# Loading the inputs of a gated linear attention a batch at a time instead of a chunk at a time

## The chip, the cores and the metric

The kernel runs on one core of one Trainium2 chip. The metric is the device time of one execution in microseconds (us), the median over several runs. Engines are named as in the profile: PE (TensorE matmuls), PEld (its weight loads), DVE (VectorE), ACT (ScalarE), POOL (GpSimd), SP (SyncE, which here only issues transfers).

## The reference

A gated linear recurrence for each of 4 batches and 8 heads over 768 steps, and an MLP mixer over its output. All inputs and the output are float32.

```python
batch, n_heads, seq, head_dim = (4, 8, 768, 48)
state = alpha[:, :, t, :, None] * state + np.einsum('bhd,bhe->bhde', k[:, :, t], v[:, :, t])
y[:, :, t] = np.einsum('bhd,bhde->bhe', q[:, :, t], state)
...
# x: y as (batch, seq, heads * head_dim) = (4, 768, 384)
xt = x.transpose(0, 2, 1)
h = np.maximum(xt @ w_tok1, 0.0) @ w_tok2        # (768, 256), (256, 768)
u = x + h.transpose(0, 2, 1)
h2 = np.maximum(u @ w_ch1, 0.0) @ w_ch2          # (384, 1536), (1536, 384)
return (u + h2).astype(np.float32)
```

## The kernel before

The sequence is cut into chunks of 128 steps, six a batch, 24 in all; n is the chunk's number, and a chunk is worked on with its 128 steps on the partitions and 8 heads x 48 channels along them. The functions of one chunk:

- `load(n)` issues four transfers on SP, one for each of `at` (alpha), `kt`, `qt` and `vt`: 128 partitions of 8 rows, a row being the 48 float32 (192 bytes) of one head and step. The tiles come from the pool `inp` with NIN = 8 buffers for each name.
- `s_ln` (L132) takes the logarithm of alpha on ACT into `la`. `s_cum` (L138 to L157) sums it over the steps with matmuls into `ps_cum`; ACT makes `a_sb` and `ia_sb` by two exponentials; POOL multiplies `kt` to `pkk` and casts `vt` to `vb`, and makes `acqm`; `qt` is multiplied to `pkq` on DVE in batch 0 and on POOL after it.
- `s_tr` (L169, L171) transposes `pkk` and `pkq` by eight matmuls into `ps_tp`, copied to `tp` (by DVE in batch 0, by ACT after it).
- `s_gt` (L180, L183) makes the 128 x 128 products `gt_ps` of the eight heads, and DVE masks them to `gtm`.
- `s_y` (L193 to L215) makes the state product `ps_s` (it uses the same one buffer as `gt_ps`), from which DVE makes the state `ss`, then the output `ps_y`, which ACT copies to `x_sb`.

The mixer of a batch needs its six `x_sb`. It is a queue of units: tok1 (L229, 12 matmuls of 128 x 384), tok2 (L238, 12, with `u_sb` by DVE), utp (L247, transposes of u to `ut`), ch1 (L259, 72 matmuls into 12 tiles `rt`, with the maximum by ACT and DVE in turn) and ch2 (L269, 72 matmuls, with `o_sb` by DVE and the store by SP at L273). `fill` emits some units behind each step of the next batch's chunks, so that PE works on batch b's mixer during batch b + 1's scan; three ch2 units of a batch are held back and put between the units of the next mixer.

A scheduler reorders what the code emits, engine by engine; every engine then runs its own list in order.

The order of transfers is partly written by hand. The weights are cast to bfloat16 by transfers that POOL issues (L112): `wt1` and `wt2` when chunk 4 of batch 0 has its `vb`, `wc1` and `wc2` when chunk 5 has. `gates[n]` is the `vb` cast of chunk n. At the start six chunks are loaded; the `at` load of chunk 6 waits for `gates[5]`, and from then on loads run seven chunks ahead. Since `kt` and `qt` of chunk 6 stand ahead of that wait on SP, they are loaded before it.

## Time and profile before

| | |
|---|---|
| time, median of 3 runs | 210.76 us (208.86 to 211.78) |
| span of the profiled execution | 208.4 us |
| its own time | not shown beside its span; the three runs lie 0.5 to 3.4 us above the span |
| mean granted TensorE clock | 0.959 |
| busy | PE 174.2 us (84%), DVE 105.0, ACT 85.8, POOL 62.9 |
| transfers | 106,322 packets, 26.99 MB, 100,288 packets under 512 bytes |
| input loads | 96 of 192 KB, 3.7 to 3.8 us from issue to landing in the median |

A row of a timeline has the start in us from the span's beginning, the length, engine, line, operation, tile written <- tiles read, shape and count; in brackets stands how long the engine was idle before it, and what ended that. A row of the waits has who waited for whom, the sum in us, how often, and the longest. Slices are fortieths of the span, 5.2 us each, in tenths.

### The profile page before, as it was taken

What the parts mean: (1) busy time and instruction counts of PE and PEld (TensorE: products, weight loads), DVE (VectorE), ACT (ScalarE), POOL (GpSimd) and SP (SyncE); (2) the same over time, 40 slices, a digit from 0 to 9 for tenths busy, and PEclk for the clock granted to TensorE, in tenths of its full rate; (3) what the DMA queues carried; (4) which work ended last, traced back from release to release, by engine and by line L of the source; (5) the groups of instructions that cost most, each with busy time, mean ns of one, the idle gap of its engine ahead of it and who ended that gap; (6) DMA issues with size and microseconds to landing.
All of it is one profiled execution on the core that took longest, in us unless ns stands there. A gap on an engine that the chain in (4) does not pass through costs nothing.

```text
span 208.4 us, 4139 instructions
## 1 busy us (share of the span) xinstructions
PE 174.2 (84%) x1616; PEld 111.5 (53%) x1616; DVE 105.0 (50%) x179; ACT 85.8 (41%) x171; POOL 62.9 (30%) x104
## 2 busy tenths in 40 slices
PE   1276669232799999989999999999999999999993
PEld 0154445111475566646666666667656665656661
DVE  1277554103357455438765664378656446555321
ACT  3442221040526773685167744642667310054000
POOL 2543166004450441583245234551444000000000
PEclk9999999958559999999999999999999999999999
DMA  7999939999999998999989802111100021110132
GB/s 142 220 220 212 182 40 175 208 182 198 191 222 218 188 223 167 226 237 212 235 198 220 165 1 78 39 38 42 38 5 0 35 82 38 40 39 0 38 113 75
DMA packets 106322, 26.99 MB, mean 129 GB/s; under 512 B 100288, under 2 KB 105920, under 8 KB 106304
## 3 DMA queue, kind: packets, MB, share of 16 engines
q1 hardware_dynamic: 103296, 23.60, 53.7%
q0 software_dynamic: 3008, 3.15, 9.2%
q8 instruction: 12, 0.20, 0.4%
q14 instruction: 6, 0.05, 0.1%
HBM read 25.17 MB, written 4.72 MB: 143 GB/s over the span
## 4 chain that ended last, share of the span: by engine, by line
PE 59%; issue 12%; DMA 10%; ACT 8%; POOL 6%; SPq 2%; DVE 1%; POOLq 0%; ACTq 0%
PE ps_mm L269 20%; PE ps_mm L259 19%; DMA at<-in_alpha_dram 10%; ACT tp L171 4%; PE ps_tp L169 4%; PE ps_mm L238 4%; PE gt_ps L180 3%; PE ps_tp L247 2%; PE ps_mm L229 2%; SPq L124 2%; PE ps_y L207 1%; ACT a_sb L144 1%; PE ps_cum L138 1%; PE gt_ps L196 1%; POOL vb L154 1%
## 5 line engine op out<-in xcount | busy, mean ns | idle before, releaser
L259 PE MATMUL ps_mm<-ut,wc_152 128*128 128x384 bf16 x288 | 53.4, 330 | 1.2 <-DVE rt L264 0.5
L269 PE MATMUL ps_mm<-wc_153,rt 128*128 128x384 bf16 x288 | 50.9, 326 | 0.0
L264 DVE TENSOR_SCALAR rt<-ps_mm 128x384 bf16<-128x384 f32 x48 | 26.5, 555 | 22.9 <-PE ps_mm L259 22.6
L183 DVE TENSOR_TENSOR gtm<-gt_ps,u_107 128x1024 bf16<-128x1024 f32 x24 | 29.3, 1220 | 15.7 <-PE gt_ps L180 15.7
L269 PEld LDWEIGHTS <-rt 128*128 128x128 bf16 x288 | 27.1, 98 | 16.9
L259 PEld LDWEIGHTS <-wc_152 128*128 128x128 bf16 x288 | 26.8, 99 | 17.4 <-issue 1.5
L262 ACT ACTIVATE rt<-ps_mm 128x384 bf16<-128x384 f32 x48 | 23.1, 497 | 23.8 <-PE ps_mm L259 23.8
L215 ACT ACTIVATE x_sb<-ps_y 128x384 bf16<-128x384 f32 x24 | 11.8, 492 | 39.3 <-PE ps_y L211 35.2
L272 DVE TENSOR_TENSOR o_sb<-ps_mm,u_sb 128x384 f32<-128x384 f32 x24 | 13.3, 556 | 28.7 <-PE ps_mm L269 28.7
L154 POOL CAST vb<-vt 128x384 bf16<-128x384 f32 x24 | 12.8, 532 | 35.4 <-issue 23.6
L171 ACT COPY tp<-ps_tp 128x1024 bf16<-128x1024 bf16 x18 | 18.3, 1017 | 7.0 <-PE ps_tp L169 6.7
L144 ACT ACTIVATE a_sb<-ps_cum 128x388 f32<-128x388 f32 x24 | 11.9, 495 | 18.6 <-PE ps_cum L141 13.0
L241 DVE TENSOR_TENSOR u_sb<-ps_mm,x_sb 128x384 bf16<-128x384 f32 x24 | 12.0, 550 | 14.2 <-PE ps_mm L238 14.0
L180 PE MATMUL gt_ps<-tp 48*128 48x128 bf16 x192 | 11.9, 241 | 4.6 <-DVE tp L171 2.4
L180 PEld LDWEIGHTS <-tp 48*128 48x128 bf16 x192 | 6.4, 102 | 13.6 <-ACT tp L171 5.9
L146 ACT ACTIVATE ia_sb<-ps_cum 128x384 f32<-128x384 f32 x24 | 11.7, 487 | 0.0
L149 POOL TENSOR_TENSOR pkk_128<-kt,ia_sb 128x384 bf16<-128x384 f32 x8 | 7.9, 993 | 11.7 <-ACT ia_sb L146 11.7
L238 PE MATMUL ps_mm<-ht,wt_151 128*128 128x384 bf16 x48 | 11.4, 374 | 0.0
L229 PE MATMUL ps_mm<-x_sb,wt_150 128*128 128x384 bf16 x48 | 10.1, 342 | 0.6 <-ACT x_sb L215 0.6
L207 PE MATMUL ps_y<-vb,gtm 128*128 128x48 bf16 x192 | 9.6, 192 | 0.9 <-DVE gtm L183 0.9
L151 POOL TENSOR_TENSOR pkq_125<-qt,a_sb 128x384 bf16<-128x384 f32 x6 | 6.0, 996 | 14.3 <-ACT a_sb L144 14.3
L157 POOL TENSOR_TENSOR acqm<-a_sb,bm 128x8 f32<-128x8 f32 x24 | 5.5, 230 | 14.9 <-ACT a_sb L144 13.8
(91 smaller groups left out, 204.3 us busy)
## 6 DMA issues: line engine op xcount, KB each, us to landing
at<-in_alpha_dram SPq DMA_DIRECT2D x24, 192.0 KB, 3.7
kt<-in_k_dram SPq DMA_DIRECT2D x24, 192.0 KB, 3.8
qt<-in_q_dram SPq DMA_DIRECT2D x24, 192.0 KB, 3.8
vt<-in_v_dram SPq DMA_DIRECT2D x24, 192.0 KB, 3.8
out_dram<-o_sb SPq DMA_DIRECT2D x24, 192.0 KB, 1.9
wc_152<-in_moe_w_ch_dram POOLq DMA_DIRECT2D x1, 1152.0 KB, 10.1
wc_153<-in_moe_w_ch_dram POOLq DMA_DIRECT2D x1, 1152.0 KB, 17.2
wt_150<-in_moe_w_tok_dram POOLq DMA_DIRECT2D x1, 384.0 KB, 5.3
```

Source lines behind the costliest of these rows:

```text
L144: act.activation(a_sb, ps_cum[:, 0 : HD + 4], AF.Exp)
L154: gates[n] = gps.tensor_copy(vb, c["vt"])
L171: (act.copy if n >= NCH else dve.tensor_copy)(tp, ps_tp)
L180: pe.matmul(gt_ps[:, 4 * (h % 2) + j, :], lhsT=tp[base : base + D, 4 + j, :], rhs=tp[base : base + D, j, :], start=True, stop=True)
L183: dve.tensor_tensor(gtm, gt_ps, mask_b, ALU.mult)
L229: pe.matmul(ps, lhsT=wt1[:, kc, m * 128 : (m + 1) * 128], rhs=x[kc], start=(kc == 0), stop=(kc == NS - 1))
L238: pe.matmul(ps, lhsT=wt2[:, kc, i * 128 : (i + 1) * 128], rhs=ht[kc], start=(kc == 0), stop=(kc == NDT - 1))
L259: pe.matmul(ps, lhsT=wc1[:, kc, mc * 128 : (mc + 1) * 128], rhs=ut[kc][:, cs], start=(kc == 0), stop=(kc == NM - 1))
L262: act.activation(t[:, cs], ps, AF.Relu)
L264: dve.tensor_scalar_max(t[:, cs], ps, 0.0)
L269: pe.matmul(ps, lhsT=rt[mc][:, i * 128 : (i + 1) * 128], rhs=wc2[:, mc, :], start=(mc == 0), stop=(mc == NDC - 1))
L272: dve.tensor_tensor(t, ps, u[i], ALU.add)
```

## The change

`load` takes a batch instead of a chunk. Each of its four transfers brings all 48 rows of a partition (8 heads x 6 chunks) into a tile whose rows stand 64 float32 (256 bytes) apart; the chunks read their part of it through a view. `inp` has 2 buffers for each name, `rt` 13 instead of 24, and `o_sb` 3 instead of 4. Batch 0 is loaded at the start, batch b + 1 at the fifth chunk of batch b. The wait on `gates[5]` stands at the `at` load of batch 1. In DRAM the rows of one head lie together, and the built program takes four of them in one piece of 768 bytes; before, each row was a piece.

```diff
-    NIN = 8
+    NIN = 2
     inp = pool("inp", NIN)
...
-    rtpool = pool("rtpool", 24)
-    opool = pool("opool", 4)
+    rtpool = pool("rtpool", 13)
+    opool = pool("opool", 3)
...
-    def load(n):
-        b, ci = divmod(n, NCH)
-        c = ctxs[n] = {"b": b, "ci": ci}
-        ts = ci * C
+    PAD = 64
+
+    def load(b):
+        ts = {}
         for name, src in (("at", alpha), ("kt", k), ("qt", q), ("vt", v)):
-            t = inp.tile([128, H, D], F32, name=name)
-            d = nc.sync.dma_start(t, src[b, :, ts : ts + C, :].transpose([1, 0, 2]))
-            if n == NCH and name == "at":
+            t = inp.tile([128, H * NCH, PAD], F32, name=name)
+            d = nc.sync.dma_start(
+                t[:, :, 0:D], src[b].rearrange("h (c p) d -> p (h c) d", p=C))
+            if b == 1 and name == "at":
                 after(d, gates[NCH - 1])
-            c[name] = t
+            ts[name] = t.rearrange("p (h c) d -> p h c d", c=NCH)
+        for ci in range(NCH):
+            c = ctxs[b * NCH + ci] = {"b": b, "ci": ci}
+            for name, t in ts.items():
+                c[name] = t[:, :, ci, 0:D]
...
-    AHEAD = NIN - 1
     if True:
-        for n in range(NCH):
-            load(n)
-        loaded = NCH
+        load(0)
...
-            while n + 1 >= NCH - 1 and loaded < min(NT, n + 1 + AHEAD):
-                load(loaded)
-                loaded += 1
+            if ci == NCH - 2 and b + 1 < B:
+                load(b + 1)
```

The scheduler's order moves with it. On PE the sums of chunks 0 to 3 now come first; a first tok1 matmul of batch 0 stands ahead of the transposes of chunk 5; all of tok2 of batch 0 stands ahead of chunk 6, and two more sums and all u transposes ahead of chunk 6's state product. On POOL the three first `vb` come after the three first `pkk`, and for batch 1 `pkq`, `acqm` and `pkk` of chunks 6 to 8 and `pkq` of chunk 9 come before the `vb` of chunk 6. On SP the stores of batch 0 and the loads of batch 3 take turns.

## The prediction

> **What bounds the kernel now.** I read the page's slices first, then two windows of the span, then the waits, and last the timeline of the first 60 us.

> ```profile
> span 208.4 us, 4139 instructions
> PE   1276669232799999989999999999999999999993
> PEclk9999999958559999999999999999999999999999
> q0 software_dynamic: 3008, 3.15, 9.2%
> HBM read 25.17 MB, written 4.72 MB: 143 GB/s over the span
> wt_150<-in_moe_w_tok_dram POOLq DMA_DIRECT2D x1, 384.0 KB, 5.3
> ```

> The windows (columns: length, then busy time and count of PE, PEld, DVE, ACT, POOL, then clock, DMA share, GB/s):

> ```profile
> 0.00:58.00 58.00, 29.71 (x280) 19.99 (x281) 23.76 (x46) 17.11 (x36) 21.24 (x40) 0.89 1.01 180
> 58.00:205.00 147.00, 144.47 (x1337) 91.52 (x1337) 80.66 (x133) 68.68 (x136) 41.69 (x64) 0.99 0.49 111
> ```

> From 58 us to 205 us PE is busy for 144.47 of 147 us: TensorE bounds that stretch, and no input load can shorten it. Before 58 us PE works for 29.71 us only, while the DMA engines are full (share 1.01). So the change is decided by when the kernel reaches the state that it has at 58 us: the first state product of batch 1 (chunk 6, L196), behind which there is always mixer work for PE. From the waits:

> ```profile
> PE ps_cum L138 <- ACT la_123 L132: 5.9, 1, 5.9
> PE ps_cum L138 <- ACT la_124 L132: 4.1, 1, 4.1
> ```

> and from the timeline:

> ```profile
> 33.29 0.37 SPq L124 DMA_DIRECT2D at<-in_alpha_dram  x1
> ...
> 38.04 0.49 ACT L215 ACTIVATE x_sb<-ps_y 128x384 bf16<-128x384 f32 x1 [4.49 <-PE ps_y L211]
> ...
> 44.43 0.52 ACT L132 ACTIVATE la_123<-at 128x384 bf16<-128x384 f32 x1 [5.89 <-DMA at<-in_alpha_dram]
> ...
> 51.96 0.52 ACT L132 ACTIVATE la_124<-at 128x384 bf16<-128x384 f32 x1 [5.44 <-DMA at<-in_alpha_dram]
> ...
> 57.97 0.50 PE L196 MATMUL gt_ps<-vb,pkk_128 128*128 128x96 bf16 x4 [0.17 <-DVE gtm L183]
> ```

> Batch 0's scan is over at 38.04 (last x_sb). Then PE waits twice, 5.9 and 4.1 us, for `at` of chunks 6 and 7: issued from 33.29 on, beside 6.3 MB of weights, they are used only at 44.43 and 51.96.

> **The change, part 1: what one batch load costs.** 96 loads of 1,024 rows become 16 of 6,144 rows; the bytes are the same. The built program reads a batch tensor in pieces of 768 bytes (four rows that lie together in DRAM) and still writes 192-byte rows, now at multiples of 256 bytes. No row of the trace has this form, so I bound it. In the window 3 to 22 us nothing runs but these loads:

> ```profile
> DMA packets 21573, 4.10 MB, mean 216 GB/s; under 512 B 21572, under 2 KB 21572, under 8 KB 21572
> ...
> 0.74 0.42 SPq L124 DMA_DIRECT2D at<-in_alpha_dram  x1
> 3.48 0.52 ACT L132 ACTIVATE la_121<-at 128x384 bf16<-128x384 f32 x1 [1.46 <-DMA at<-in_alpha_dram]
> ```

> 16 engines x 19 us / 21,572 = 14.1 ns for a row on its engine. A batch tensor is 384 rows per engine: D = 5.4 us if nothing changes for the row. The other end: the weights are 25.17 - 18.87 (the inputs) = 6.3 MB of long reads in 9.2% of 208.4 us = 19.2 us, 328 GB/s; at that rate 1.18 MB take D = 3.6 us. The reads come nearer to the weights', the writes stay as they were, so I take the middle, D = 4.5 us. The first load took 2.74 us, of which 0.9 us are its 64 rows per engine; the fixed part is 1.84 us, so `at`, `kt`, `qt`, `vt` of batch 0 land at 2.6 + D, 2D, 3D, 4D: 7.1, 11.6, 16.1 and 20.6 us.

> [...]

> **Part 2: batch 0's scan starts later.** Now chunk 0 can't begin before all six chunks of a tensor are there. The durations, from chunk 0 of before (its timeline):

> ```profile
> 8.12 0.56 DVE L151 TENSOR_TENSOR pkq_125<-qt,a_sb 128x384 bf16<-128x384 f32 x1 [6.27 <-ACT a_sb L144]
> ...
> 9.75 0.61 PE L169 MATMUL ps_tp<-id_112,pkk_128 128*128 128x128 bf16 x4 [0.67 <-POOL pkk_128 L149]
> ...
> 10.23 1.00 POOL L149 TENSOR_TENSOR pkk_129<-kt,ia_sb 128x384 bf16<-128x384 f32 x1
> ...
> 10.82 0.69 DVE L171 COPY tp<-ps_tp 128x1024 bf16<-128x1024 bf16 x1 [0.62 <-PE ps_tp L169]
> 11.17 0.50 POOL L154 CAST vb<-vt 128x384 bf16<-128x384 f32 x1
> 11.57 0.60 PE L180 MATMUL gt_ps<-tp 48*128 48x128 bf16 x8 [0.79 <-DVE tp L171]
> ...
> 12.29 1.23 DVE L183 TENSOR_TENSOR gtm<-gt_ps,u_107 128x1024 bf16<-128x1024 f32 x1 [0.78 <-PE gt_ps L180]
> ...
> 13.57 0.48 PE L196 MATMUL gt_ps<-vb,pkk_128 128*128 128x96 bf16 x4
> ...
> 14.16 0.56 DVE L201 TENSOR_TENSOR ss_131<-gt_ps,acqm 128x384 bf16<-128x384 f32 x1
> 14.16 0.20 POOL L157 TENSOR_TENSOR acqm<-a_sb,bm 128x8 f32<-128x8 f32 x1 [2.49 <-ACT a_sb L144]
> 14.41 0.49 ACT L215 ACTIVATE x_sb<-ps_y 128x384 bf16<-128x384 f32 x1
> ```

> In the changed program's order `qt`, landing at Q = 2.6 + 3D, is what starts the chain: three pkq on DVE (1.7), tp 0.7, gt 0.65, gtm 1.25, so Q + 4.4 with the gaps; then tp, pkq and the transposes of chunk 2 stand ahead of the first state product on DVE and PE (2.0): Q + 6.4. `vt` lands at Q + D, so vb is there by Q + 5.0 and hidden. The state needs 0.9 from its product to ss, and 0.6 for ss: Q + 8.0. From there a chunk takes gt 0.65 + gtm 1.25 + 0.9 + ss 0.6 + gaps = 3.6: chunk 1's ss and y are over at Q + 12, vb and acqm of chunk 4 at Q + 12.8, and there POOL issues the first weights.

> ```profile
> 27.73 1.00 POOL L112 DMA_DIRECT2D wt_150<-in_moe_w_tok_dram  x1
> ...
> 33.27 1.16 PE L229 MATMUL ps_mm<-x_sb,wt_150 128*128 128x384 bf16 x3
> ```

> Their landing takes 5.3 us: Q + 18.1. In the new order one tok1 matmul, which reads wt1, stands on PE ahead of chunk 5's transposes, so the scan stops there until then. Two transposes (1.2), five tok1 (5 x 0.39 = 1.9) and the rounds of chunks 3, 4 and 5 (state, gt, gtm: 0.9 + 0.6 + 0.65 + 1.25 twice, and y) end the scan at Q + 29.2, which is 45.3 us against 38.04. Two tok1 matmuls, the ht copy and six u_sb follow:

> ```profile
> 46.58 2.16 DVE L241 TENSOR_TENSOR u_sb<-ps_mm,x_sb 128x384 bf16<-128x384 f32 x4 [9.18 <-PE ps_mm L238]
> ...
> 52.53 0.48 PE L138 MATMUL ps_cum<-la_124,u_107 128*128 128x384 bf16 x1 [4.07 <-ACT la_124 L132]
> 52.81 0.29 PE L141 MATMUL ps_cum<-ones_col,la_124 128*128 128x1 bf16 x4
> ```

> 6 x 0.54 = 3.3, so tok2 ends at T = Q + 33.4 = 49.5 us.

> **Part 3: batch 1 is there earlier.** `kt` and `qt` of batch 1 are no longer two chunks ahead of the gate but six: they follow `vt` at once and land by 2.6 + 6D = 29.6 us, while the weights are issued at 28.9. `at` (still gated by vb of chunk 5, Q + 16.2 = 32.3) and `vt` come beside the weights. All transfers up to there: 2.6 + 8D + 19.2/1.08 = 56.4 us, where 1.08 is the sum of the two shares in the window 34 to 44:

> ```profile
> q0 software_dynamic: 852, 1.54, 87.0%
> q1 hardware_dynamic: 1464, 0.28, 20.7%
> ```

> All of tok2 now precedes chunk 6 on PE, so the 5.9 and 4.1 us waits are filled. From T: ps_cum 0.6, exponential 0.5, then POOL does pkq, acqm and pkk (2.2) for three chunks, the pkq of chunk 9 (1.0) and only then vb of chunk 6 (0.5; its source now has gaps, at most the 1.0 of pkk): the state product of chunk 6 at T + 9.6 = 59.1 us, where it was 57.97. `vt` allows 56.4 + 0.6 = 57.0, so it is hidden by 2 us. By then PE has done more than before at its 57.97: two more ps_cum (1.1) and

> ```profile
> 58.62 0.81 PE L247 MATMUL ps_tp<-id_112,u_sb 128*128 128x128 bf16 x6
> ```

> six u transposes, part of it at either clock: 1.5 us credit.

> **Edits that I cost at nothing.** 13 rt tiles: ch2 of a batch precedes ch1 of the next in the new PE order, so the tiles are free; without that order 12 matmuls (2 us) a batch would wait. Three o_sb: they are made 2 us apart, a store lands in 1.9; a store behind a batch load would wait D, which three buffers nearly cover (under 1 us). 80 fewer issues on SP: SP is on no wait that PE sees. Loads of batches 2 and 3: with the old or the new D they are over long before their scans.

> **Sum.** 59.1 - 58.0 - 1.5 = -0.4 us; the hand-made chain ignores collisions of DVE with POOL, for which I add 1 us: +0.6, span 209.0. The shown times of before (208.86 to 211.78, median 210.76) lie 0.5 to 3.4 around its span; against the median I say 211.4 us. Two per cent, 4.2 us, is about what a measurement of this kernel tells from no change.

> **Rivals.**

> (a) *Slower: `at` of batch 1 starves.* It decides once `at` lands after T = 49.5. In the window 34 to 44 us q1 moved 0.28 MB beside the weights, and in 44 to 52 us

> ```profile
> q1 hardware_dynamic: 3629, 0.69, 54.2%
> ```

> 0.69 MB. At those rates 1.18 MB issued at 32.3 land at 52.8, and chunk 6's product comes at 52.8 + 0.5 + 9.6 = 62.9: +4.4 with the other terms, 215.2 us. [...]

> (b) *Slower: the change doesn't do what it says.* The rows still cost 14.1 ns: D = 5.4, Q = 18.8, transfers end at 63.6, and `vt` then ends last: product at 64.2, +5.7 with 1 us for collisions: 216.5 us. For it: the writes are as many and as short as before.

> (c) *Faster.* D = 3.6 and PE at full rate: the 0.48 and 0.29 rows are about twice what the same matmuls cost after 62 us; work packed behind `qt` may keep PE fast. Q = 13.4, a round costs 0.7 less (five of them) and the last chain 1.5 less: product at 13.4 + 43.0 - 5.0 = 51.4 (transfers allow 49.8): -8.1 + 1 = -7.1, 203.7 us. Against it: PE waits between the steps of every chunk as before.

> **How the numbers follow.** Forecast (within 2%) 0.43; (a) 0.23, (b) 0.14, (c) 0.20. A part of (a) and (b) lies under 4.2 us, but worse mixtures of both are as likely: faster 0.20, same 0.43, slower 0.37. The range reaches from (c) to (b) and a little past it: 204.0 to 218.0 us; the forecast's own is 207 to 215 (3D moves by 2.7 us either way when D goes to its ends, and the collisions by 1).

> **What would show it.** Right: the stretch from the first chunk-6 state product to the end is 150 us as now; that product at 57 to 61 us; first x_sb near 24 us (14.41 before); last x_sb of batch 0 near 45; a landing of 4 to 5 us per batch tensor; no PE wait on o_sb or rt. Wrong: PE waiting on `at` after tok2 (a), on vb of chunk 6 behind `vt` (b), or a stall after 65 us, which no part above has.

## The result, and the profile after

The changed kernel takes 224.53 us in the median (223.95 to 225.11) against 211.02 (208.86 to 211.78): 1.067 times the time, with a 95% interval of 1.061 to 1.073. Its profiled execution took 224.29 us with a span of 222.5; the span grew by 14.1 us. The mean granted clock is 0.959, as before.

The page of the changed kernel, its slices:

```profile
span 222.5 us, 4016 instructions
PE   0031358428666899999999999999999999999993
PEclk9999999999676599999999999999999999999999
DMA  5999999999999999997998792210200020110022
GB/s 110 163 163 164 163 163 164 165 203 226 232 220 163 167 164 168 163 167 179 189 157 192 140 173 37 73 36 35 75 1 3 0 74 35 71 38 0 35 90 89
```

PE's full stretch begins at slice 14 of 40 (78 us, a slice being 5.6 us here), where it began at slice 11 (57 us). The DMA engines are busy from the start, but while only inputs move they carry 163 GB/s, where they carried some 216. The window 3 to 22 us says it in rows: each packet is four rows now.

```profile
DMA packets 4119, 3.14 MB, mean 165 GB/s; under 512 B 32, under 2 KB 4119, under 8 KB 4119
```

The timeline of the changed kernel, to the first state product of chunk 6:

```profile
10.55 1.76 ACT L137 ACTIVATE la<-at 128x384 bf16<-128x384 f32 x4 [8.54 <-DMA at<-in_alpha_dram]
...
17.82 2.90 POOL L154 TENSOR_TENSOR pkk<-kt,ia_sb 128x384 bf16<-128x384 f32 x3 [1.81 <-DMA kt<-in_k_dram]
...
22.42 6.75 SPq L124 DMA_DIRECT2D kt<-in_k_dram  x1
...
25.07 1.50 DVE L156 TENSOR_TENSOR pkq<-qt,a_sb 128x384 bf16<-128x384 f32 x3 [23.22 <-DMA qt<-in_q_dram]
...
29.62 6.76 SPq L124 DMA_DIRECT2D qt<-in_q_dram  x1
...
32.27 1.40 POOL L159 CAST vb<-vt 128x384 bf16<-128x384 f32 x3 [11.55 <-DMA vt<-in_v_dram]
...
33.66 0.49 ACT L220 ACTIVATE x_sb<-ps_y 128x384 bf16<-128x384 f32 x1 [3.54 <-PE ps_y L212]
...
38.45 1.71 POOL L112 DMA_DIRECT2D wt<-in_moe_w_tok_dram  x2
...
48.94 0.50 PE L234 MATMUL ps_mm<-x_sb,wt 128*128 128x384 bf16 x1 [7.42 <-DMA wt<-in_moe_w_tok_dram]
...
58.97 0.49 ACT L220 ACTIVATE x_sb<-ps_y 128x384 bf16<-128x384 f32 x1 [2.40 <-PE ps_y L216]
...
60.57 4.00 PE L243 MATMUL ps_mm<-ht,wt 128*128 128x384 bf16 x12 [0.26 <-ACT ht L237]
...
64.55 1.35 ACT L137 ACTIVATE la<-at 128x384 bf16<-128x384 f32 x3 [3.65 <-DMA at<-in_alpha_dram]
...
74.81 0.53 PE L201 MATMUL gt_ps<-vb,pkk 128*128 128x96 bf16 x4
```

The four tensors of batch 0 are first used at 10.55, 17.82, 25.07 and 32.27: 7.2 us apart, so D is 7.2 us, or 18.8 ns for each of an engine's 384 rows (14.1 before). The first x_sb comes at 33.66 instead of 14.41, the state product of chunk 6 at 74.81 instead of 57.97. From there to the end of the span are 147.7 us, before 150.4. The waits of the changed kernel:

```profile
PE ps_cum L143 <- ACT la L137: 11.7, 2, 11.1
PE ps_mm L234 <- DMA wt<-in_moe_w_tok_dram: 7.4, 1, 7.4
PE ps_tp L174 <- DVE pkq L156: 6.2, 1, 6.2
```

All three lie before 75 us: the wait for `at` at the start (and 0.6 us for that of batch 1), the wait for wt1, and the wait for `qt` behind pkq. So the time was lost before the state product of chunk 6, where it was expected to be decided, and there the rows are slower. The experiments ask first why a row got slower, then what is left without that.

### The profile page after: what moved, and what is told of

Same layout as the page of the kernel before. It is cut to its first block, busy times and chain, and to the rows that moved or that the text cites. A ratio compares the mean times of both kernels' runs of the same rounds, so it can differ in the third digit from the quotient of the medians.

```text
span 222.5 us, 4016 instructions
## 1 busy us (share of the span) xinstructions
PE 175.1 (79%) x1616; PEld 113.0 (51%) x1616; DVE 103.8 (47%) x179; ACT 85.3 (38%) x171; POOL 61.3 (28%) x104
## 3 DMA queue, kind: packets, MB, share of 16 engines
q0 software_dynamic: 3008, 3.15, 8.6%
HBM read 25.17 MB, written 4.72 MB: 134 GB/s over the span
## 4 chain that ended last, share of the span: by engine, by line
PE 57%; SPq 13%; issue 11%; DMA 8%; ACT 7%; DVE 1%; POOL 1%; ACTq 0%; POOLq 0%
PE ps_mm L274 21%; PE ps_mm L264 17%; SPq L124 13%; DMA qt<-in_q_dram 8%; ACT tp L176 3%; PE gt_ps L185 3%; PE ps_mm L243 3%; PE ps_tp L174 3%; PE ps_tp L252 2%; PE ps_mm L234 2%; PE ps_y L212 1%; ACT rt L267 1%; PE ps_cum L143 1%; PE gt_ps L201 1%; ACT a_sb L149 1%
## 5 line engine op out<-in xcount | busy, mean ns | idle before, releaser
L264 PE MATMUL ps_mm<-ut,wc 128*128 128x384 bf16 x288 | 53.6, 330 | 1.2 <-ACT rt L267 0.5
L274 PE MATMUL ps_mm<-wc,rt 128*128 128x384 bf16 x288 | 51.3, 326 | 0.0
L188 DVE TENSOR_TENSOR gtm<-gt_ps,u 128x1024 bf16<-128x1024 f32 x24 | 29.3, 1221 | 16.6 <-PE gt_ps L185 16.6
L264 PEld LDWEIGHTS <-wc 128*128 128x128 bf16 x288 | 26.8, 99 | 17.6 <-issue 2.0
L156 POOL TENSOR_TENSOR pkq<-qt,a_sb 128x384 bf16<-128x384 f32 x18 | 18.0, 999 | 58.6 <-ACT a_sb L149 45.1
L220 ACT ACTIVATE x_sb<-ps_y 128x384 bf16<-128x384 f32 x24 | 11.8, 490 | 52.5 <-PE ps_y L216 45.3
L154 POOL TENSOR_TENSOR pkk<-kt,ia_sb 128x384 bf16<-128x384 f32 x24 | 23.8, 996 | 10.6 <-PE gt_ps L201 5.2
L176 ACT COPY tp<-ps_tp 128x1024 bf16<-128x1024 bf16 x18 | 18.3, 1017 | 8.4 <-PE ps_tp L174 8.3
L149 ACT ACTIVATE a_sb<-ps_cum 128x388 f32<-128x388 f32 x24 | 11.8, 494 | 21.8 <-PE ps_cum L146 11.2
L206 DVE TENSOR_TENSOR ss<-gt_ps,acqm 128x384 bf16<-128x384 f32 x20 | 11.1, 554 | 15.2 <-PE gt_ps L201 15.2
L234 PE MATMUL ps_mm<-x_sb,wt 128*128 128x384 bf16 x48 | 11.0, 363 | 8.0 <-DMA wt<-in_moe_w_tok_dram 7.4
L137 ACT ACTIVATE la<-at 128x384 bf16<-128x384 f32 x24 | 11.8, 526 | 12.2 <-DMA at<-in_alpha_dram 12.2
L174 PE MATMUL ps_tp<-id,pkq 128*128 128x128 bf16 x96 | 11.1, 246 | 6.2 <-DVE pkq L156 6.2
## 6 DMA issues: line engine op xcount, KB each, us to landing
wt<-in_moe_w_tok_dram POOLq DMA_DIRECT2D x2, 384.0 KB, 11.2
at<-in_alpha_dram SPq DMA_DIRECT2D x4, 0.2 KB, 14.9
kt<-in_k_dram SPq DMA_DIRECT2D x4, 0.2 KB, 16.2
```

Source lines behind the costliest of these rows:

```text
L149: act.activation(a_sb, ps_cum[:, 0 : HD + 4], AF.Exp)
L154: gps.tensor_tensor(pkk[:, :, 0:D], c["kt"], ia_sb.rearrange("p (h d) -> p h d", h=H), ALU.mult)
L156: qeng.tensor_tensor(pkq[:, :, 0:D], c["qt"], a_sb[:, 0:HD].rearrange("p (h d) -> p h d", h=H), ALU.mult)
L174: pe.transpose(ps_tp[:, 4 * w + j, :], src[:, 2 * j : 2 * j + 2, :], id128)
L176: (act.copy if n >= NCH else dve.tensor_copy)(tp, ps_tp)
L188: dve.tensor_tensor(gtm, gt_ps, mask_b, ALU.mult)
```

## The experiments

### Which part of the new load makes a row slow

Four parts of the change were taken apart: the read of four rows in a piece (theory A), the gaps (B), the partitions that are written at once (C), and the batch itself.

**Each tensor in two transfers by heads.** Each half is 0.59 MB, and the built program reads every row of it by itself again; the rows stay 256 bytes apart.

```diff
-            d = nc.sync.dma_start(
-                t[:, :, 0:D], src[b].rearrange("h (c p) d -> p (h c) d", p=C))
+            R = H * NCH // 2
+            for i in range(2):
+                d = nc.sync.dma_start(
+                    t[:, i * R : (i + 1) * R, 0:D],
+                    src[b, i * H // 2 : (i + 1) * H // 2].rearrange(...))
```

> The changed kernel with each batch tensor loaded by two transfers, heads 0 to 3 and heads 4 to 7. Each is under 1 MiB, and in the built program every row of 192 bytes is a piece of its own again; the rows still stand 256 bytes apart, and the rest is as changed. Theory A (the pieces of four rows are what made a batch tensor cost 7.2 us): a tensor is back at 5.4 us or less, 14.1 ns a row or less; by the prediction's own sum the first state product of chunk 6 is then near 62 us (74.8 in the changed kernel) and the time near 213 us, 11 under the changed kernel. Theory B (the gaps between the rows cost): still near 7.2 us a tensor, 223 to 226 us. [...]

Measured: 224.68 us, ratio 1.071 (1.067 to 1.076). Its window 3 to 22 us:

```profile
DMA packets 16340, 3.12 MB, mean 164 GB/s; under 512 B 16340, under 2 KB 16340, under 8 KB 16340
```

These are single rows, at the same 164 GB/s: theory A falls.

**No gaps.** The changed kernel with `PAD = 48`; the pieces of four rows stay.

> The changed kernel with the rows side by side in SBUF (a pitch of 192 instead of 256 bytes), still read in pieces of four rows. Theory A (pieces of four rows cost): no better than 7.2 us a tensor, and worse if gaps help the writes: 7.2 to 9 us, time 224 to 236 us. Theory B (gaps cost): 5.4 us a tensor or less, time 210 to 216 us.

Measured: 213.89 us (one run), span 212.1. Its window 3 to 22 us:

```profile
DMA packets 5536, 4.21 MB, mean 222 GB/s; under 512 B 48, under 2 KB 5536, under 8 KB 5536
```

The rate is back, and 10.6 us of the loss are gone with the gaps. Three tensors lie between the first use of `at` and that of `vt`:

```profile
8.84 1.76 ACT L137 ACTIVATE la<-at 128x384 bf16<-128x384 f32 x4 [6.82 <-DMA at<-in_alpha_dram]
...
25.04 1.40 POOL L159 CAST vb<-vt 128x384 bf16<-128x384 f32 x3 [7.87 <-DMA vt<-in_v_dram]
```

That makes D 5.4 us.

**Halves by partitions.** The changed kernel with each tensor in two transfers of 64 partitions.

> The changed kernel with each batch tensor loaded by two transfers, partitions 0 to 63 and 64 to 127; every row is a piece of its own, 256 bytes apart. [...] Theory A (the long read with its four writes is slow by itself): the same cost as with halves by heads, 5.4 us or less, and a time near 213 us.

Measured: 162 GB/s (16,134 rows in the window). Theory C fits that, but theory B does as well, so this run does not tell them apart. The two runs above do: the halves by heads are read row by row, into all 128 partitions, and were as slow, and the pieces of four rows were fast without gaps. So theory C falls by those. The time is 246.94 us (one run); where the 22 us beyond the changed kernel arise was not followed up.

**No gaps and halves by heads.**

> The changed kernel with rows 192 bytes apart and two transfers by heads for each batch tensor, so that every row is its own piece. If reading four rows in one piece is worth nothing in itself: 14.1 ns a row and 213 to 215 us, as with the one long transfer without gaps (213.9 us in one run). If it is worth something: 14.5 to 15 ns a row and 1 to 3 us more than that.

Measured: 215.68 us, ratio 1.027 (1.020 to 1.033), 221 GB/s. Without gaps, four rows in a piece change nothing in the rate either (222 against 221 GB/s). The time is 1.8 us above the single run of the long transfers; why was not followed up.

### The gaps in the kernel before

Here the kernel before keeps its loads by chunk, and only its tiles change:

```diff
-            t = inp.tile([128, H, D], F32, name=name)
+            t = inp.tile([128, H, 64], F32, name=name)[:, :, 0:D]
```

> The kernel before with its chunk loads, rows 256 bytes apart in SBUF: the spacing alone. If the spacing does nothing: 14.1 ns a row and the time of before within 0.5%. If it costs (theory B): 18 ns a row, and some 6 to 12 us more, since the first 52 us of before are bound by transfers. [...]

Measured: 212.97 us, ratio 1.013 (1.008 to 1.018). Its window 3 to 22 us:

```profile
DMA packets 16618, 3.14 MB, mean 165 GB/s; under 512 B 16618, under 2 KB 16618, under 8 KB 16618
```

These are the same slow rows (18.3 ns), at a smaller price than expected: 2.9 us instead of 6 to 12. The state product of chunk 6 comes at 60.93 us, 3.0 us later than in the kernel before. Then other pitches (a pitch is the distance from row to row): 224 bytes (56 instead of 64), and 320 bytes (80, with 13 `rt` and three `o_sb` to make room).

> The kernel before with its chunk loads, rows 224 bytes apart in SBUF (192 in before: 14.1 ns a row; 256: 18.9 ns). Theory B1 (any gap between the written rows costs): near 18.9 ns a row. Theory B2 (a multiple of 256 costs, every row of a partition then starting at the same place of a 256-byte line): near 14.1 ns. Theory B3 (the cost goes with the distance, 0.0735 ns a byte in both known cases): 16.5 ns. Time 210 to 213 us in all of them; the window from 3 to 22 us tells.

> The kernel before with rows 320 bytes apart, 13 rt tiles and 3 o_sb tiles (for room). B1 (any gap): near 18.9 ns a row. B2 (multiples of 256): near 14.1 ns. B3 (by distance): 23.5 ns, and a time of 216 us or more.

Measured: 210.69 us at 205 GB/s, and 209.54 us at 212 GB/s (one run each), which is 14.9 and 14.3 ns a row. Gaps alone cost next to nothing, and theory B2 came nearest. And the two small pools (`rtpool` 13, `opool` 3) alone:

> The kernel before with 13 rt and 3 o_sb tiles alone. The prediction costed both at nothing: within 0.5% of before. Rival: the fewer buffers make PE wait at each batch's end (2 us a batch, three batches): 2 to 3% more.

Measured: 210.07 us, ratio 0.9998 (0.997 to 1.003).

So 256 was the price, it seemed. Then a pitch of 256 with the row 64 bytes later in its place:

```diff
-            t = inp.tile([128, H, D], F32, name=name)
+            t = inp.tile([128, H, 64], F32, name=name)[:, :, 16:64]
```

> The kernel before with rows at a pitch of 256 bytes, as in the padded run, but each row begins 64 bytes past a multiple of 256. Theory P (the pitch of 256 costs, wherever the row lies in its 256 bytes): window 3 to 22 us at about 165 GB/s, 18.3 ns a row, time about 213. Theory S (a row that begins on a multiple of 256 costs): 205 to 216 GB/s, 14 to 15 ns a row, time about 210.

Measured: 209.32 us (one run). Its window 3 to 22 us:

```profile
DMA packets 20653, 3.92 MB, mean 206 GB/s; under 512 B 20652, under 2 KB 20652, under 8 KB 20652
```

That is the rate of rows without gaps in the runs beside it (205 and 206 GB/s). So it is not the pitch alone, but where the row starts. In the built program the input tiles begin at byte 54,464 of a partition, which is 212 x 256 + 192. The rows of the changed kernel therefore all start 192 bytes past a multiple of 256 and run over the next one; the offset run's rows start on it. Theory S as I had worded it, a price for rows that begin on a multiple, has it the wrong way round.

### Where the row starts

One line moves all input tiles of the changed kernel: 64 unused bytes make its rows start on multiples of 256, 128 bytes make it 64 past one, 192 make it 128 past one.

```diff
     ss_t = [fix.tile([128, H, D], BF16, name=f"ss{i}") for i in range(NSS)]
+    fix.tile([128, 16], F32, name="shift")
```

> The changed kernel with 64 unused bytes ahead of its input tiles. In the program as built these tiles begin at byte 54,464 of a partition, 192 past a multiple of 256, so every row of the changed kernel starts 192 bytes past such a multiple and runs over the next one; here all start on one. [...] Rival R (a row costs 14 ns at best, whatever its start): 216 to 222 GB/s and 213 to 215, as without gaps.

> The same with 192 unused bytes: all rows start 128 bytes past a multiple of 256 and still run over the next one. [...] Rival X (running over a multiple of 256 costs the same wherever the row starts): 165 GB/s and about 224.

> The changed kernel with 128 unused bytes ahead of its input tiles: all rows start 64 bytes past a multiple of 256 and end on the next one, without running over it. Theory X (a row pays for running over a multiple of 256, wherever it starts): as with rows on the multiples, about 253 GB/s in the window 3 to 22 us, 12 ns a row, time about 212. [...]

Measured: start 0 takes 212.02 us, ratio to before 1.011 (1.009 to 1.013); start 128 takes 224.09 and start 64 takes 211.27 (one run each). The window 3 to 22 us of start 0 (GB/s in 40 slices of 0.475 us), of start 128, of start 64:

```profile
GB/s 204 297 335 307 309 320 281 168 186 189 257 323 306 322 315 312 230 65 191 223 243 297 317 327 317 315 212 116 278 230 296 306 319 320 319 259 55 58 189 197
DMA packets 6316, 4.80 MB, mean 253 GB/s; under 512 B 64, under 2 KB 6316, under 8 KB 6316
```

```profile
DMA packets 4177, 3.18 MB, mean 168 GB/s; under 512 B 32, under 2 KB 4177, under 8 KB 4177
```

```profile
DMA packets 6387, 4.86 MB, mean 256 GB/s; under 512 B 64, under 2 KB 6387, under 8 KB 6387
```

Starts 0 and 64 agree (253 and 256 GB/s), and so do 128 and 192 (168 and 165): what counts is whether the row runs over a multiple of 256 (theory X of the last expectation). Rival R, with 216 to 222 GB/s at start 0, missed. Between the dips, where one transfer ends and the next begins, start 0 moves some 316 GB/s: 192 x 16 / 316 = 9.7 ns a row. The changed kernel's 163 GB/s are 18.8 ns, about twice as much. Rows without gaps start at 192, 128, 64 and 0 in turn, so two of four run over a multiple: the mean of 9.7 and 18.8 is 14.3 ns, and 13.8 were measured (222 GB/s, four rows in a piece). At the pitch of 224, five of eight run over: 15.4 by the same account, and 14.9 were measured.

In the kernel before, whose rows are read one by one, that account does not hold as it stands. All rows running over took 18.3 ns there and none running over (the offset run) 14.7, which is no less than rows without gaps took. So something other than the row's place limits the rate there; what it is, no run shows.

Last, start 0 with each tensor in two transfers by heads (single rows read):

> The changed kernel with 64 unused bytes ahead of its input tiles (rows on multiples of 256) and each tensor in two transfers by heads, which makes the program read every row by itself instead of four in a piece. Theory M (the row costs the longer of its read and its write, and a row read by itself costs 14 to 15 ns): 206 to 216 GB/s and a time of 213 to 216, as without gaps. Rival N (reading four rows in a piece is worth nothing, as it was without gaps): 250 to 255 GB/s and about 212.

Measured: 214.59 us (one run). Its window 3 to 22 us:

```profile
DMA packets 23142, 4.42 MB, mean 233 GB/s; under 512 B 23142, under 2 KB 23142, under 8 KB 23142
```

Between the two theories: 13.1 ns a row, against 12.1 with four rows in a piece. With rows that stay within 256 bytes the longer pieces are worth something (253 to 233 GB/s), with the others they were not (165 to 164). How much of the difference is the read, and how much the doubled number of transfers, is open. (The offset run in the kernel before, with single rows in transfers of a sixth of the size and as well on multiples of 256, had 14.7 ns.)

### What is left without the slow rows

**The changed order with transfers by chunk** (no gaps, 12 tiles of each name, loads of a batch issued together at the same places):

```diff
+        for ci in range(NCH):
+            ...
+                t = inp.tile([128, H, D], F32, name=name)
+                d = nc.sync.dma_start(t, src[b, :, ts : ts + C, :].transpose([1, 0, 2]))
```

> The order of the changed kernel (a batch's loads issued together at the same places, 13 rt, three o_sb), but each tensor of a batch comes in six transfers, one a chunk, in tiles without gaps. Only the waiting for a whole batch tensor is taken away, and the gaps with it. Theory W (waiting for the whole batch is what is left of the loss when the gaps are gone): last x_sb of batch 0 near 38 us and a time of 208 to 211. Rival O (the order in which the parts of PE's work stand is what is left): 213 to 216, as with whole batch transfers without gaps.

Measured: 210.09 us, ratio 1.001 (0.999 to 1.004), and the last x_sb of batch 0 is at 38.51, as theory W had it. The changed order costs nothing that can be told from noise here. Without gaps, whole batch tensors took 213.89 us (one run), 3.8 us more, which I put down to the waiting for a whole batch. With rows on multiples of 256, 1.1% over the kernel before is left (start 0).

**The wait on `gates[5]`.** The kernel before without it:

```diff
-            if n == NCH and name == "at":
-                after(d, gates[NCH - 1])
```

> The kernel before, without the wait of chunk 6's first input (`at`) for vb of chunk 5; the 8 loads of chunks 6 and 7 then follow those of batch 0 at once. Theory G (the gate is what makes PE wait in the kernel before): the 5.9 and 4.1 us waits of PE for `la` of chunks 6 and 7 go, the first state product of chunk 6 comes from 57.97 us to 48 to 51, and the time is 202 to 205 us against 210. Rival (the weights need those engines): the 8 loads take about 9 us of full DMA, the weights land later, the token matmuls of batch 0 wait for them, and the time is 209 to 213.

Measured: 205.80 us, ratio 0.979 (0.976 to 0.982). The waits for chunks 6 and 7 are gone, but the chunk-6 product comes at 53.41, not the 48 to 51 expected: of the two waits for `la` in the first row one is that at the start (4.3), the other, of 4.6 us, is new and belongs to chunk 8, whose loads are issued later. The waits of this run:

```profile
PE ps_cum L136 <- ACT la L130: 8.9, 2, 4.6
...
PE ps_mm L227 <- DMA wt<-in_moe_w_tok_dram: 1.2, 1, 1.2
```

and from its timeline:

```profile
52.41 0.52 ACT L130 ACTIVATE la<-at 128x384 bf16<-128x384 f32 x1 [4.95 <-DMA at<-in_alpha_dram]
...
53.41 0.48 PE L194 MATMUL gt_ps<-vb,pkk 128*128 128x96 bf16 x4
```

The same lines taken out of the run with chunk transfers in the changed order, and out of the changed kernel with rows on multiples of 256:

> The run with one transfer a chunk in the changed kernel's order, and also without the wait of batch 1's first input for vb of chunk 5. Theory G: batch 1's inputs are there before its scan starts, PE does not wait for them, time 202 to 206. Rival (24 loads now stand ahead of or beside the weights): the weights land some 10 us later, PE waits for wt1 and wc1, and the time is 210 to 216.

> The changed kernel with rows on multiples of 256 and without the wait of batch 1's first input for vb of chunk 5. If both gains add up: all of batch 1 lands before the weights, which land at most 5 us later than with the gate; time 202 to 207. Rival: the weights come later and hold the scan of batch 0, 208 to 212.

Measured: 204.62 us in the median of three runs (a fourth, at 207.00, is not in the ratio), ratio 0.973 (0.967 to 0.978), and 204.25 us, ratio 0.976 (0.973 to 0.980). Both lie in the range of the theory that stands first (202 to 206 and 202 to 207). The last run puts batch 0 into the batch tiles by chunk, without the gate:

> The run before this, but batch 0's tensors come in six transfers each, one a chunk, into the same tiles. Batch 0's scan then starts as early as in the kernel before (first x_sb near 14.5 us), and batch 1 comes in whole transfers at 4.1 to 4.4 us each: 199 to 205, below the 205.0 of chunk transfers alone. Rival: the start of batch 0 is hidden by the weights' landing anyway, same time as the run before this.

Measured: 210.98 us, ratio 1.007 (1.004 to 1.009). Both theories miss. The 4.1 to 4.4 us for a batch tensor, on which the first of them stands, no run shows; with start 0 it was 4.6. Its first x_sb is at 14.74, as early as before, but batch 1 comes later: `kt` and `qt` are issued from 24.67 on and now share the engines with the weights of 28.07, and the scan of batch 1 waits for `qt`:

```profile
24.67 4.56 SPq L126 DMA_DIRECT2D kt<-in_k_dram  x1
...
28.07 1.71 POOL L113 DMA_DIRECT2D wt<-in_moe_w_tok_dram  x2
...
29.68 8.24 SPq L126 DMA_DIRECT2D qt<-in_q_dram  x1
...
55.14 3.87 POOL L159 TENSOR_TENSOR pkq<-qt,a_sb 128x384 bf16<-128x384 f32 x4 [2.46 <-DMA qt<-in_q_dram]
...
63.97 0.53 PE L204 MATMUL gt_ps<-vb,pkk 128*128 128x96 bf16 x4
```

The chunk-6 product is at 63.97, later than in any of the other ungated profiles read here. An earlier batch 0 bought nothing, because batch 1 decides. Batch 0 by chunk is read row by row and moves 206 GB/s in the window 3 to 22 us, where the run before it moved 255 and issued batch 1's `kt` at 20.32.

## Why the prediction was wrong, point by point

Two kernels are read here: the changed one, whose timeline stands above, and the run with start 0, whose rows lie where the prediction had them. The timeline of start 0:

```profile
7.38 1.76 ACT L138 ACTIVATE la<-at 128x384 bf16<-128x384 f32 x4 [5.36 <-DMA at<-in_alpha_dram]
...
16.62 1.50 DVE L157 TENSOR_TENSOR pkq<-qt,a_sb 128x384 bf16<-128x384 f32 x3 [14.76 <-DMA qt<-in_q_dram]
...
29.35 1.71 POOL L113 DMA_DIRECT2D wt<-in_moe_w_tok_dram  x2
...
34.66 0.50 PE L235 MATMUL ps_mm<-x_sb,wt 128*128 128x384 bf16 x1 [2.23 <-DMA wt<-in_moe_w_tok_dram]
...
45.65 3.57 PE L244 MATMUL ps_mm<-ht,wt 128*128 128x384 bf16 x12 [0.42 <-ACT ht L238]
...
52.30 1.35 ACT L138 ACTIVATE la<-at 128x384 bf16<-128x384 f32 x3 [6.32 <-DMA at<-in_alpha_dram]
...
62.57 0.53 PE L202 MATMUL gt_ps<-vb,pkk 128*128 128x96 bf16 x4
```

- **The step that failed** is part 1: "still writes 192-byte rows, now at multiples of 256 bytes", and with it the bounds of D. The rows do not stand there: the tiles begin 192 bytes past a multiple. I took the place of a row from its pitch and never asked for the tile's address, which the built program shows. So D was taken as 4.5 with 5.4 "if nothing changes for the row" as the worst, and measured 7.2. In the kernel before two of four rows run over a multiple, in the changed kernel all four, so a loss was possible where I excluded one. The range ended at 218 for that reason.
- With the rows where the prediction had them (start 0) D is (16.62 - 7.38) / 2 = 4.6 us and the time 212.0, against 4.5 and 211.4 forecast. So the loss above that, 224.5 - 212.0 = 12.5 us, is the size of this one term and what hangs on it. Of the 4.6 us of D, 384 x 9.7 ns = 3.7 are rows; the rest shows as the dips in the slices between transfers.
- **The chain behind `qt`** held when the measured D is put in: wt1 is issued at Q + 13.4 (12.8 forecast). The scan's end and tok2 went with it, up to the weights: T came 15.6 us after the weights were there, 15.3 forecast.
- **The weights' landing** was the second term mis-sized: 5.3 us taken, 10.5 measured (38.45 to 48.94), because batch 1's `kt` and `qt`, issued from 22.42 on at 7.2 us each, still ran. With rows on multiples it is 5.3 (29.35 to 34.66), so it too follows from D.
- **From T to the product** 9.6 us were forecast and 10.2 measured (64.57 to 74.81). The credit after it is 2.7 us instead of 1.5 (147.7 us to the end instead of 150.4).
- **Part 3, `at` of batch 1 hidden**, did not hold even at the forecast's D. With start 0 tok2 ends at 49.22 (45.65 + 3.57), but `at` is used at 52.30 only, and the product comes at 62.57. That is rival (a): it had `at` at 52.8 and the product at 62.9. The end came to 212.0 rather than its 215.2, since the stretch after the product was 147.6 us, 2.8 shorter than before, and the collisions that I added did not show. So where the forecast's number was nearly met, it was by luck: the product was 3.5 us later than forecast, and the shorter stretch and the collisions made up 2.3 of them. In the changed kernel itself the same wait is 3.65 us on ACT and 0.6 on PE, because tok2 was late too.
- **Rival (b)** (D = 5.4, 216.5 us) is the run without gaps: D is 5.4 and the time 213.9 (one run). It was the nearest of the four to the truth in kind, a row that gets no faster, and still too mild.
- **Rival (c)** misread its rows. After 62 us the matmuls of 0.48 and 0.29 us take 0.33 and 0.24, so they were 1.5 and 1.2 times as long, not twice, and no run shows that packed work keeps PE fast:

```profile
68.18 0.33 PE L138 MATMUL ps_cum<-la_122,u_107 128*128 128x384 bf16 x1
68.34 0.24 PE L141 MATMUL ps_cum<-ones_col,la_122 128*128 128x1 bf16 x4
```

- **Edits at nothing** (13 `rt`, three `o_sb`): right, 0.9998.

## What to carry to other kernels

Before costing a padded layout, work out the absolute address of each row (tile base plus pitch), and count the rows that run over a multiple of 256: here those cost 18.8 ns and the others 9.7 when four rows were read in a piece. Read one by one, the others still took 13.1 to 14.7, so the place alone gained little there over rows without gaps (13.8 to 14.8). Bound an unmeasured transfer on the side of a loss as well, and above all where the rows it is compared with stand at several places within their 256 bytes. A load that is made coarser or earlier only pays if the next load on the path moves too: what gained here was one wait taken off batch 1's first input (0.973 to 0.979), in three layouts of the four in which the wait was taken out. In the fourth, batch 1's `qt` came late and nothing was gained (1.007).

## What the runs showed of the hardware that I had not expected

The granted clock is not settled by these runs. These are the clock rows of start 0 with the wait on `gates[5]` and without it:

```profile
PEclk9999999988557999999999999999999999999998
```

```profile
PEclk9999999999999999999999999999999999999999
```

The first has a mean of 0.957, the second of 1.0. But the wait alone does not decide it: the kernel before with rows 256 bytes apart keeps the wait and had 1.0 in its profiled run (0.943 to 0.959 in its other three), and the run with batch 0 by chunk has no wait and had 0.948 to 0.949 in all four. Nor is the clock all that shortens the stretch from chunk 6's product to the end. With the wait and without it, the windows of that stretch are:

```profile
62.57:210.20 147.63, 142.34 (x1321) 90.35 (x1319) 80.74 (x133) 65.10 (x128) 38.69 (x61) 0.99 0.29 88
```

```profile
58.16:201.40 143.24, 138.42 (x1293) 87.73 (x1292) 79.14 (x130) 62.80 (x123) 37.95 (x60) 1.00 0.32 97
```

It is 4.4 us shorter without the wait, but 28 of its matmuls then already lie before the product, and the clock in it is 1.00 against 0.99. What makes the clock fall was not tried.
